# Windowed attention and eight experts on one core: the second expert product in plain f32, with tokens stationary

## The chip, the core and the metric

The kernel runs on one NeuronCore of a Trainium2 chip. Five engines work side by side: TensorE (PE in the rows; its weight loads are PEld), VectorE (DVE), ScalarE (ACT), GpSimd (POOL) and SyncE (SP, which here only starts transfers). The metric is the device time of one execution in microseconds; lower is better. All inputs lie in device memory in the layouts that the host prepares, and one launch does everything.

## The reference, cut to what matters

Eight batches of eight heads attend over a causal window of 64 positions. The result is laid out as 4608 tokens of 512 features, each token is sent to one of eight experts, and an expert keeps its 80 tokens of largest gate weight; all other rows of the output are zero.

```python
scores = scale * np.matmul(q, k.transpose(0, 1, 3, 2))     # 8 x 8 x 576 x 576, window of 64
attn = softmax(np.where(mask, scores, -1e9))
x = (attn @ v).transpose(0, 2, 1, 3).reshape(4608, 512)
expert_idx = np.argmax(x @ w_gate, axis=1)
for e in range(8):
    tok_idx = the 80 tokens of expert e with the largest gate weight
    h = np.maximum(x[tok_idx] @ w1[e], 0.0)                # 80 x 1024
    out[tok_idx] = gate_w[tok_idx, None] * (h @ w2[e])     # 80 x 512
```

## The kernel before

**Attention.** The tokens are worked on in 36 blocks of 128 (`unit`, `half`, `tail`): scores on TensorE in four tiles of 64 rows by 64 columns (L337), masking and maximum on VectorE (L350), the subtraction on GpSimd (L355), the exponential on ScalarE (L357), transposes (L366), the product with v in two column tiles (L417), then another transpose and the gate's logits in four column tiles of 32 (L444). Each finished block is written to `x_dram` (L379), and zeros are written to its rows of the output (L389). A routine called `list_schedule` works out beforehand in which order every engine's instructions are written down, from estimated durations; DMAs that SyncE starts are one of its queues. In it the first expert's weights are loaded in eight pieces of 512 KB (`first_weights`, L395 and L398). For a batch of 9 units of 64 tokens, q and k (L271) and v (L296, L302) are loaded into two buffers each, and GpSimd copies parts of v (L155).

**Routing** runs alongside and ends after the last block: ranks per expert in groups of blocks (`weigh`, `gate`, `merge`), and at the end `kept` (L585 to L598) with the list of 8 times 80 rows. While TensorE has little to do there, a job called `warm` puts in matmuls of an all-zero bf16 tile that nobody reads (L719). Another 28 of these (`WARM2`, L809) are written behind the gathers.

**Experts.** `gather` fetches an expert's 80 rows with an indirect DMA (L742), `load_x` turns them with four transposes (L769) and a copy (L770) so that features lie on partitions. `ffn1` computes h turned: the weights are stationary in two column tiles of 64, the 80 tokens stream past (64 matmuls in f32, each of which stands twice in the trace, L781). `ffn2` computes 80 tokens by 512 features with h stationary. It does not use f32 matmuls: `split` cuts w2 into a rounded part `wh` (ScalarE, L758) and the rest `wl` (VectorE, L759), h is cut in the same way (L783, L784), and three fp32r products per chunk of 128 are added up, 24 matmuls of 512 columns (L797). VectorE scales by the gate weight (L799), and an indirect DMA scatters the rows (L800). Two sets of weight buffers are in turn; expert e+2's load waits until expert e is done with its set. The order on TensorE is: transposes of e+1, second product of e, first product of e+1.

## Time and profile before

| | |
|---|---|
| median of 3 runs | 313.46 us (310.69 to 316.4) |
| the profiled execution | 313.2 us |
| its span, first to last instruction | 311.3 us |
| mean granted TensorE clock | 0.974 of full |
| TensorE busy | 279.2 us, 90% |
| moved by DMA | 84.32 MB |

The span falls into attention with routing beside it (to about 200 us), the end of the routing (to 214 us), the gather of the first expert's rows (to 217.7 us), and the experts (to 307 us), with the last scatter behind them. Times in the rows are microseconds from the start of the span. A matmul's own duration includes the way through the array, so matmuls that follow each other overlap, and the distance of their starts is what one costs.

### The profile page before, as it was taken

Reading aid. Unit: us, or ns where it says so; the run is one execution under the profiler, and the core shown is the slowest. Engines: PE = TensorE matmul, PEld = TensorE weight load, DVE = VectorE, ACT = ScalarE, POOL = GpSimd, SP = SyncE. Lnnn points to the kernel's source line nnn. Section 1 sums busy time; section 2 is a strip of 40 time slices with the busy share of each in tenths; the row PEclk is TensorE's granted clock in tenths of the full one; section 3 lists DMA queues with packets and bytes.
Section 4 is the critical chain, followed back from the end, with each engine's and each line's share of the span. In section 5 each row is a group of like instructions: output and inputs, shape, how many; then the busy total and the mean of one; then the engine's idle time right before and its main releaser. Section 6 shows DMA issues by size and latency. Waiting matters only on the chain. (4 is left out here: it accounts for less than half of the span.)

```text
span 311.3 us, 11705 instructions
## 1 busy us (share of the span) xinstructions
PE 279.2 (90%) x4706; PEld 221.2 (71%) x4706; DVE 220.6 (71%) x1084; ACT 157.2 (51%) x305; POOL 160.0 (51%) x255
## 2 busy tenths in 40 slices
PE   7699999888989998889997998895999999999983
PEld 5478787666866876667875876663977886787683
DVE  1358665677749857999799998984686466595471
ACT  1263876666565545766575667320555055145320
POOL 8899878698589579769766242003700101110111
PEclk9789999999999999999999999998699999999998
DMA  7978599889899958398371313991898999999400
GB/s 275 428 260 330 213 335 369 302 275 373 285 343 335 321 201 306 138 364 316 114 265 72 137 71 137 301 373 36 287 344 273 412 430 368 394 430 400 179 23 21
DMA packets 22245, 84.32 MB, mean 271 GB/s; under 512 B 2352, under 2 KB 2480, under 8 KB 18608
## 3 DMA queue, kind: packets, MB, share of 16 engines
q1 hardware_dynamic: 20736, 76.70, 66.4%
q10 hardware_dynamic: 432, 4.26, 4.2%
q0 software_dynamic: 1024, 2.62, 2.7%
q8 instruction: 37, 0.61, 0.8%
q14 instruction: 16, 0.13, 0.1%
HBM read 63.39 MB, written 20.19 MB: 269 GB/s over the span
## 5 line engine op out<-in xcount | busy, mean ns | idle before, releaser
L355 POOL TENSOR_TENSOR sm<-nb,sm 128x512 f32<-128x512 f32 x72 | 74.3, 1040 | 23.7 <-DVE nb L350 8.7
L357 ACT ACTIVATE sm<-sm 128x512 f32<-128x512 f32 x72 | 44.9, 633 | 37.5 <-POOL sm L355 37.1
L366 PE MATMUL pT_ps<-ident,sm 128*128 128x128 f32 x288 | 43.8, 284 | 5.9 <-ACT sm L357 4.9
L369 ACT COPY pT<-pT_ps 128x512 f32<-128x512 f32 x72 | 40.8, 586 | 11.6 <-PE pT_ps L366 11.0
L800 POOL DMA_INDIRECT out_dram<-y,dst_i x8 | 7.3, 919 | 75.8 <-DVE y L799 75.8
L759 DVE TENSOR_TENSOR wl<-w2t,wh 128x1024 fp32r<-128x1024 f32 x28 | 32.4, 1221 | 19.3 <-ACT wh L758 19.3
L337 PE MATMUL sc<-qkT 64*64 64x128 f32 x1152 | 42.7, 280 | 2.2 <-DVE nb L350 2.1
L155 POOL TENSOR_SCALAR vw<-vw 64x520 f32<-64x520 f32 x64 | 39.7, 621 | 9.4 <-DMA vw<-in_v_dram 5.9
L417 PE MATMUL o<-vw,pT 128*64 128x65 f32 x1152 | 42.3, 226 | 0.0
L417 PEld LDWEIGHTS o<-vw,pT 128*64 128x64 f32 x1152 | 37.2, 139 | 7.0 <-issue 5.3
L366 PEld LDWEIGHTS pT_ps<-ident,sm 128*128 128x128 f32 x288 | 32.8, 144 | 11.1 <-ACT sm L357 6.4
L337 PEld LDWEIGHTS sc<-qkT 64*64 64x64 f32 x1152 | 33.0, 135 | 9.2 <-issue 7.3
L758 ACT CAST wh<-w2t 128x1024 fp32r<-128x1024 f32 x28 | 27.2, 1046 | 15.4 <-DMA w2t<-in_w_dram 15.4
L350 DVE CUSTOM_DVE_ANT_0 sm<-sc,mask_oe 128x128 f32<-128x128 f32 x128 | 29.1, 286 | 6.8 <-PE sc L337 5.8
L781 PEld LDWEIGHTS hp<-xgT,w1t 128*64 128x64 f32 x896 | 31.4, 137 | 2.7 <-ACT wh L758 1.6
L781 PE MATMUL hp<-xgT,w1t 128*64 128x80 f32 x896 | 32.5, 233 | 0.0
L439 ACT COPY xT<-xT_ps 128x512 f32<-128x512 f32 x36 | 21.0, 583 | 19.7 <-PE xT_ps L436 19.4
L797 PE MATMUL yp<-wh,hh 128*80 128x512 f32 (+1 forms) x72 | 26.8, 372 | 1.0 <-DVE hh L783 0.9
L350 DVE CUSTOM_DVE_ANT_0 sm<-sc,mask_eo 128x128 f32<-128x128 f32 x96 | 21.8, 285 | 8.0 <-PE sc L337 7.9
L797 PE MATMUL yp<-wl,hh 128*80 128x512 f32 (+1 forms) x72 | 26.4, 367 | 0.0
L797 PE MATMUL yp<-wh,hl 128*80 128x512 f32 (+1 forms) x72 | 26.4, 367 | 0.0
L436 PE MATMUL xT_ps<-ident,xt 128*128 128x128 f32 x144 | 22.6, 279 | 3.6 <-DVE g L519 1.4
(132 smaller groups left out, 447.3 us busy)
## 6 DMA issues: line engine op xcount, KB each, us to landing
w1t<-in_w_dram SPq DMA_DIRECT2D x6, 2048.0 KB, 9.3
w2t<-in_w_dram SPq DMA_DIRECT2D x6, 2048.0 KB, 13.8
x_dram<-xt SPq DMA_DIRECT2D x36, 256.0 KB, 3.8
out_dram<-zeros SPq DMA_DIRECT2D x36, 256.0 KB, 4.4
qkT<-in_qk_dram SPq DMA_DIRECT2D x7, 1280.0 KB, 6.8
vw<-in_v_dram SPq DMA_DIRECT2D x7, 1040.0 KB, 6.7
qkT<-in_qk_dram SPq DMA_DIRECT2D x7, 1024.0 KB, 8.9
w<-in_w_dram SPq DMA_DIRECT2D x8, 512.0 KB, 6.6
```

The lines of the kernel that those rows point to most:

```text
L155: nc.gpsimd.tensor_scalar(dst, src, 1.0, 1.0, op0=ALU.mult, op1=ALU.mult)
L337: nc.tensor.matmul(scs[T][r][64 * m:64 * m + 64, pr, :], qkT[b][hp, i, pr, 0, :], kw, start=True, stop=True, tile_position=(64 * r, 64 * m))
L350: nc.vector.tensor_tensor_reduce(sm[:, pr], scs[T][r][:, pr], mask, op0=ALU.add, op1=ALU.min, scale=-0.125, scalar=-8.0 * NEG, accum_out=n ...
L355: nc.gpsimd.tensor_tensor(sm, nb.unsqueeze(2).broadcast_to([P, NP, P]), sm, op=ALU.subtract)
L357: nc.scalar.activation(sm, sm, AF.Exp)
L366: nc.tensor.transpose(tp[:, pr, :], sm[:, pr, :], ident)
L369: nc.scalar.copy(pT, tp)
L417: nc.tensor.matmul(ov[64 * m:64 * m + 64, h // 4, h % 4, :], pTs[T, h % 2][:, h // 2, 64 * m:64 * m + 64], vw[b][:, i, h, :], start=True, ...
L758: nc.scalar.copy(wh[:, f:f + 2, :], ws[e][1][:, f:f + 2, :])
L759: nc.vector.tensor_tensor(wl[:, f:f + 2, :], ws[e][1][:, f:f + 2, :], wh[:, f:f + 2, :].bitcast(F32), op=ALU.subtract)
L781: nc.tensor.matmul(hp[64 * m:64 * m + 64, f, :], ws[e][0][:, c, col:col + 64], xTs[e][:, c, :], start=(c == 0), stop=(c == KD - 1), tile_p ...
L797: nc.tensor.matmul(yp[:, 0:w], a[:, f, :], b[:, f, c:c + w], start=(f == 0 and i == 0), stop=(f == KF - 1 and i == 2))
```

## The change

The second product is taken in f32 from the unsplit w2. The tokens in h stay stationary. The first 64 of them go into the two halves of TensorE's columns, where half m produces output features 256 m to 256 m + 255 (`ya`); the other 16 go into the four quarters, where quarter m produces features 128 m to 128 m + 127 (`yb`). `split`, the second tile of h and the buffers for `wh` and `wl` are gone. VectorE scales the two halves; ScalarE scales the four quarters into rows 64 to 79. For that the gate weights are copied once to the partitions on which the parts come out (`gwa`, `gwb`). There are four sets of weights instead of two: the second expert's set is loaded during attention like the first, in eight more pieces. The first product of expert e+1 and the transposes of e+2 come ahead of the second product of e. The 28 matmuls of zeros are written by `warm` behind the end of the routing.

```diff
-    w_first = (w0.tile([P, KD, F], F32, name="w1_0"), w0.tile([P, KF, DM], F32, name="w2_0"))
+    w_first = [(w0.tile([P, KD, F], F32, name=f"w1_{i}"), w0.tile([P, KF, DM], F32, name=f"w2_{i}")) for i in range(2)]
...
         def first_weights(i):
-            yield f"?spill{i + 6}"
+            e, i = divmod(i, KD + KF // 2)
+            yield f"?spill{i + 6 + 10 * e}"
...
-        for i in range(KD + KF // 2):
+        for i in range(2 * (KD + KF // 2)):
             jobs.append((2 * i + 24, first_weights(i)))
...
+            left = WARM2
             for _ in range(1000 if end else WARM0):
-                if "kept" in state:
+                left -= "kept" in state
+                if left < 0:
                     break
...
-    wr = ctx.enter_context(tc.tile_pool(name="wr", bufs=2, reuse_waits="tile"))
+    ws = w_first + [(wt.tile([P, KD, F], F32, name=f"w1_{i}"), wt.tile([P, KF, DM], F32, name=f"w2_{i}"))
+                    for i in range(2, 4)]
...
     def weights(e, eng=nc.sync):
+        for t, w in zip(ws[e % len(ws)], (w1, w2)):
+            eng.dma_start(t, w[e])
...
-    def split(e, f0, f1):
...
-        nc.vector.tensor_scalar(hh[:, f0:f0 + 4, :], hp, 0.0, None, op0=ALU.max)
-        nc.vector.scalar_tensor_tensor(hl[:, f0:f0 + 4, :], hp, 0.0, hh[:, f0:f0 + 4, :].bitcast(F32),
-                                       op0=ALU.max, op1=ALU.subtract)
+        nc.vector.tensor_scalar(hs[e][:, f0:f0 + 4, :], hp, 0.0, None, op0=ALU.max)

     def ffn2(e):
...
-        w = DM if e + 1 < E else DM // 2
-        for c in range(0, DM, w):
-            yp = ps_y.tile([n_, DM], F32, name="yp")
+        def product(yp, k, x0, x1):
+            n = DM * k // P
             for f in range(KF):
-                for i, (a, b) in enumerate(((hh, wh), (hh, wl), (hl, wh))):
-                    nc.tensor.matmul(yp[:, 0:w], a[:, f, :], b[:, f, c:c + w], start=(f == 0 and i == 0),
-                                     stop=(f == KF - 1 and i == 2))
-            nc.vector.tensor_scalar(y[:, c:c + w], yp[:, 0:w], gw[:, e:e + 1], None, op0=ALU.mult)
+                for m in range(P // k):
+                    nc.tensor.matmul(yp[k * m:k * m + x1 - x0, :], h[:, f, x0:x1], w[:, f, n * m:n * m + n],
+                                     start=(f == 0), stop=(f == KF - 1), tile_position=(0, k * m))
+
+        product(ya, 64, 0, 64)
+        nc.vector.tensor_scalar(y[0:64, 0:DM // 2], ya[0:64], gw[0:64, e:e + 1], None, op0=ALU.mult)
+        nc.vector.tensor_scalar(y[0:64, DM // 2:DM], ya[64:128], gwa[64:128, e:e + 1], None, op0=ALU.mult)
+        product(yb, 32, 64, n_)
+        for m in range(4):
+            part = slice(32 * m, 32 * m + n_ - 64)
+            nc.scalar.activation(y[64:n_, P * m:P * m + P], yb[part], AF.Copy, scale=gwb[part, e:e + 1])
...
     with tc.manual_schedule():
-        weights(1)
+        weights(2)
         for e in range(E):
             gather(e)
-        t = ps_w.tile([P, 512], F32, name="warm")
-        for _ in range(WARM2):
-            nc.tensor.matmul(t[:, 0:WARMN], idle[:, 0:P], idle, start=True, stop=True)
         load_x(0)
...
         ffn1(0, 0)
-        split(0, 4, KF)
         ffn1(0, 4)
+        load_x(1)
         for e in range(E):
-            if e + 1 < E:
-                load_x(e + 1)
-                split(e + 1, 0, KF)
-            if 0 < e < E - 2:
-                weights(e + 2)
-            ffn2(e)
             if e + 1 < E:
                 ffn1(e + 1, 0)
                 ffn1(e + 1, 4)
+            if e + 2 < E:
+                load_x(e + 2)
+            ffn2(e)
+            if e + len(ws) < E:
+                weights(e + len(ws))
```

TensorE near the end of the routing, before. L719 and L809 are the matmuls of zeros, L444 the gate's logits, L675 a transpose of the routing:

```order
L719 LDWEIGHTS idle
L719 MATMUL warm<-idle 128x256
L444 MATMUL lg<-xT,wgp 32x128 x4
L809 LDWEIGHTS idle
L809 MATMUL warm<-idle 128x256
...
L675 LDWEIGHTS st
L675 MATMUL vp<-ident_b,st 24x80
```

The 28 of L809, though written behind the gathers, stand between the routing's matmuls in the built program; only three of L719 stand behind the routing's last one. The same place and the place behind the routing's last matmul (L663) in the changed program, on the same engine, where L722 writes all matmuls of zeros:

```order
L722 LDWEIGHTS idle
L722 MATMUL warm<-idle 128x256
L445 MATMUL lg<-xT,wgp 32x128 x4
L676 LDWEIGHTS st
L676 MATMUL vp<-ident_b,st 24x80
...
L663 MATMUL ns<-st,oho 80x6
L722 LDWEIGHTS idle
L722 MATMUL warm<-idle 128x256
...
L766 MATMUL tp<-ident,xg 128x80 x4
```

None of the 28 stands between the routing's matmuls now; 31 stand in a row behind the last one, ahead of the first expert's transposes (L766).

TensorE in the experts, before (tp are transposes, hp a first product, yp a second):

```order
L769 MATMUL tp<-ident,xg 128x80 x4
L781 MATMUL hp<-xgT,w_0_145 64x80 x64
L769 MATMUL tp<-ident,xg 128x80 x4
L797 MATMUL yp<-wh,hh 80x512
L797 MATMUL yp<-wl,hh 80x512
L797 MATMUL yp<-wh,hl 80x512
...
L781 MATMUL hp<-xgT,w1t 64x80 x64
```

And in the changed program, from the first expert's transposes on:

```order
L766 MATMUL tp<-ident,xg 128x80 x4
L777 MATMUL hp<-xgT,w_0_145 64x80 x64
L766 MATMUL tp<-ident,xg 128x80 x4
L777 MATMUL hp<-xgT,w_1_147 64x80 x64
L766 MATMUL tp<-ident,xg 128x80 x4
L791 MATMUL ya<-w_0_146,h 64x256 x16
L791 MATMUL yb<-w_0_146,h 16x128 x32
L777 MATMUL hp<-xgT,w_2_4606 64x80 x64
```

Two first products now stand ahead of the first second product, with one set of transposes straight ahead of the second of them; every later set of transposes has a second product behind it.

SyncE's queue in the middle of attention in the changed program (L396 and L399 are the pieces of the second expert's weights, the others as before):

```order
L379 DMA x_dram<-xt 128x512
L396 DMA w_1_147<-in_w_dram 128x1024
L389 DMA out_dram<-zeros 128x512
L379 DMA x_dram<-xt 128x512
L271 DMA qkT<-in_qk_dram 128x2560
L379 DMA x_dram<-xt 128x512
L271 DMA qkT<-in_qk_dram 128x2048
L396 DMA w_1_147<-in_w_dram 128x1024
L399 DMA w_1_148<-in_w_dram 128x1024
```

The eight new pieces stand between the blocks' writes, the loads of q, k and v and the zeros, and some of the zeros stand later than before. On VectorE and ScalarE the order of attention and routing is unchanged; on TensorE one set of transposes and on GpSimd one copy of v stands a place earlier.

## Rows read from the trace of the kernel before

**Rows 1.** The head of the page: span, busy time of each engine, and the granted clock in tenths in 40 slices of 7.8 us.

```profile
span 311.3 us, 11705 instructions
PE 279.2 (90%) x4706; PEld 221.2 (71%) x4706; DVE 220.6 (71%) x1084; ACT 157.2 (51%) x305; POOL 160.0 (51%) x255
...
PEclk9789999999999999999999999998699999999998
```

**Rows 2.** Busy time by stretch: start and end, length, busy time (and instructions) of PE, PEld, DVE, ACT and POOL, then the granted clock, the DMA's share and GB/s. First a part of the attention, then the experts 1 to 6.

```profile
100.00:150.00 50.00, 45.24 (x880) 36.24 (x875) 41.81 (x258) 30.80 (x67) 39.18 (x59) 1.00 0.74 266
...
224.00:290.00 66.00, 65.88 (x986) 51.49 (x981) 45.60 (x59) 26.14 (x31) 6.40 (x7) 1.00 0.98 382
```

**Rows 3.** The same columns in short stretches around the end of the routing.

```profile
207.00:209.00 2.00, 1.72 (x14) 0.93 (x13) 1.86 (x13) 0.71 (x3) 0.00 (x0) 1.00 1.01 434
214.30:216.00 1.70, 0.00 (x0) 0.00 (x0) 0.60 (x5) 0.00 (x0) 1.29 (x2) 1.00 0.00 0
216.00:218.00 2.00, 0.34 (x3) 0.37 (x4) 0.00 (x0) 0.00 (x0) 1.69 (x2) 0.57 0.52 137
220.00:222.00 2.00, 2.00 (x36) 2.00 (x34) 1.55 (x2) 2.00 (x3) 1.70 (x2) 0.50 0.78 287
224.00:226.00 2.00, 2.00 (x48) 1.82 (x43) 2.00 (x3) 0.14 (x1) 0.88 (x1) 1.00 1.13 385
```

**Rows 4.** Instructions in order of time at the hand-over to the experts: start, duration, engine, line, operation, and in brackets the idle time ahead of it with what ended it.

```profile
213.76 0.49 PE L719 MATMUL warm<-idle 128*128 128x256 bf16 x3
214.40 1.16 POOL L742 DMA_INDIRECT xg<-x_dram,src_i  x1 [24.18 <-DVE val L587]
217.66 0.77 PE L769 MATMUL tp<-ident,xg 80*128 80x80 f32 x4 [3.41 <-DMA xg<-x_dram,src_i]
218.24 0.29 ACT L770 COPY xgT<-tp 128x160 f32<-128x160 f32 x1 [7.04 <-PE tp L769]
218.58 6.81 PE L781 MATMUL hp<-xgT,w 128*64 128x80 f32 x128 [0.16 <-ACT xgT L770]
225.33 0.50 PE L769 MATMUL tp<-ident,xg 80*128 80x80 f32 x4
```

**Rows 5.** The same view for one undisturbed expert: its first product, transposes, the first and the last matmul of the second product, and the next expert's first product.

```profile
241.79 4.65 PE L781 MATMUL hp<-xgT,w1t 128*64 128x80 f32 x128
246.37 0.50 PE L769 MATMUL tp<-ident,xg 80*128 80x80 f32 x4
246.66 0.44 PE L797 MATMUL yp<-wh,hh 128*80 128x512 f32 x1
246.96 0.43 ACT L770 COPY xgT<-tp 128x320 f32<-128x320 f32 x1 [6.32 <-PE tp L769]
251.77 0.39 PE L797 MATMUL yp<-wl,hh 128*80 128x512 f32 x1
252.00 0.39 PE L797 MATMUL yp<-wh,hl 128*80 128x512 f32 x1
252.32 4.65 PE L781 MATMUL hp<-xgT,w1t 128*64 128x80 f32 x128
```

**Rows 6.** f32 matmuls in column tiles during attention, in order of time: 128 columns past four tiles of 128 rows by 32 columns (L444) and of 64 by 64 (L337), and what follows them on TensorE.

```profile
103.78 0.64 PE L444 MATMUL lg<-xT,wgp 128*32 128x128 f32 x16
...
109.16 0.43 PE L444 MATMUL lg<-xT,wgp 128*32 128x128 f32 x8
109.52 1.10 PE L337 MATMUL sc<-qkT 64*64 64x128 f32 x32
110.56 0.33 PE L452 MATMUL lg<-ident,ls 128*128 128x128 f32 x1
```

**Rows 7.** Groups of instructions, by line and form: count, then busy time and mean duration (ns) of one, then idle time ahead of them and what ended it. VectorE's part of the splits, two f32 matmuls in column tiles, and a small copy on ScalarE.

```profile
L759 DVE TENSOR_TENSOR wl<-w2t,wh 128x1024 fp32r<-128x1024 f32 x28 | 32.4, 1221 | 19.3 <-ACT wh L758 19.3
L781 PE MATMUL hp<-xgT,w1t 128*64 128x80 f32 x896 | 32.5, 233 | 0.0
L337 PE MATMUL sc<-qkT 64*64 64x128 f32 x1152 | 42.7, 280 | 2.2 <-DVE nb L350 2.1
L450 ACT COPY ls<-lg 128x128 f32<-128x128 f32 x4 | 1.0, 262 | 2.5 <-PE lg L444 2.5
```

**Rows 8.** The last two experts in order of time, to the last scatter.

```profile
283.92 4.65 PE L781 MATMUL hp<-xgT,w1t 128*64 128x80 f32 x128
294.76 4.65 PE L781 MATMUL hp<-xgT,w1t 128*64 128x80 f32 x128
300.32 0.32 PE L797 MATMUL yp<-wh,hh 128*80 128x256 f32 x1 [0.91 <-DVE hh L783]
306.08 0.28 PE L797 MATMUL yp<-wh,hl 128*80 128x256 f32 x1
306.40 0.48 DVE L799 TENSOR_SCALAR y<-yp,gw 80x256 f32<-80x256 f32 x1 [2.31 <-PE yp L797]
307.16 0.91 POOL L800 DMA_INDIRECT out_dram<-y,dst_i  x1 [6.19 <-DVE y L799]
```

**Rows 9.** Transfers by kind: count, size of one, and median time from issue to landing; w2t are the second halves of the later experts' weights, w the pieces of the first expert's.

```profile
w2t<-in_w_dram SPq DMA_DIRECT2D x6, 2048.0 KB, 13.8
w<-in_w_dram SPq DMA_DIRECT2D x8, 512.0 KB, 6.6
```

**Rows 10.** Who waited for whom: GpSimd's copies of v for the load; us in total, times, longest.

```profile
POOL vw L155 <- DMA vw<-in_v_dram: 5.9, 5, 2.2
```

More of the change, by code (lines that the diff above doesn't have):

```diff
@@ L729, in attn_moe @@
     src_i, dst_i, gw = state["kept"]
-    wt = ctx.enter_context(tc.tile_pool(name="wt", bufs=2, reuse_waits="tile"))
-    wr = ctx.enter_context(tc.tile_pool(name="wr", bufs=2, reuse_waits="tile"))
+    wt = ctx.enter_context(tc.tile_pool(name="wt", bufs=1, reuse_waits="tile"))
     fk = ctx.enter_context(tc.tile_pool(name="fk", bufs=2, reuse_waits="tile"))
@@ L735, in attn_moe @@
     ps_y = ctx.enter_context(tc.tile_pool(name="ps_y", bufs=2, space=PSUM))
-    ps_w = ctx.enter_context(tc.tile_pool(name="ps_w", bufs=1, space=PSUM))
+    ps_z = ctx.enter_context(tc.tile_pool(name="ps_z", bufs=2, space=PSUM))
     n_ = CAP
-    xgs, ws, hs, xTs, wsp = {}, {0: w_first}, {}, {}, {}
+    xgs, hs, xTs = {}, {}, {}
+    ws = w_first + [(wt.tile([P, KD, F], F32, name=f"w1_{i}"), wt.tile([P, KF, DM], F32, name=f"w2_{i}"))
+                    for i in range(2, 4)]
+    gwa = fk.tile([P, E], F32, name="gwa", bufs=1)
+    gwb = fk.tile([P, E], F32, name="gwb", bufs=1)
     def gather(e):
@@ L746, in weights @@
     def weights(e, eng=nc.sync):
-        w1t = wt.tile([P, KD, F], F32, name="w1t")
-        eng.dma_start(w1t, w1[e])
-        w2t = wt.tile([P, KF, DM], F32, name="w2t")
-        eng.dma_start(w2t, w2[e])
-        ws[e] = w1t, w2t
-    def split(e, f0, f1):
-        if f0 == 0:
-            wsp[e] = (wr.tile([P, KF, DM], F32R, name="wh"), wr.tile([P, KF, DM], F32R, name="wl"))
-        wh, wl = wsp[e]
-        for f in range(f0, f1, 2):
-            nc.scalar.copy(wh[:, f:f + 2, :], ws[e][1][:, f:f + 2, :])
-            nc.vector.tensor_tensor(wl[:, f:f + 2, :], ws[e][1][:, f:f + 2, :], wh[:, f:f + 2, :].bitcast(F32),
-                                    op=ALU.subtract)
+        for t, w in zip(ws[e % len(ws)], (w1, w2)):
+            eng.dma_start(t, w[e])
     def load_x(e):
@@ L773, in ffn1 @@
         if f0 == 0:
-            hs[e] = (fk.tile([P, KF, n_], F32R, name="hh"), fk.tile([P, KF, n_], F32R, name="hl"))
-        hh, hl = hs[e]
+            hs[e] = fk.tile([P, KF, n_], F32, name="h")
         hp = ps_h.tile([P, 4, n_], F32, name="hp")
@@ L780, in ffn1 @@
                     col = P * (f0 + f) + 64 * m
-                    nc.tensor.matmul(hp[64 * m:64 * m + 64, f, :], ws[e][0][:, c, col:col + 64], xTs[e][:, c, :],
+                    nc.tensor.matmul(hp[64 * m:64 * m + 64, f, :], ws[e % len(ws)][0][:, c, col:col + 64], xTs[e][:, c, :],
                                      start=(c == 0), stop=(c == KD - 1), tile_position=(0, 64 * m))
-        nc.vector.tensor_scalar(hh[:, f0:f0 + 4, :], hp, 0.0, None, op0=ALU.max)
-        nc.vector.scalar_tensor_tensor(hl[:, f0:f0 + 4, :], hp, 0.0, hh[:, f0:f0 + 4, :].bitcast(F32),
-                                       op0=ALU.max, op1=ALU.subtract)
+        nc.vector.tensor_scalar(hs[e][:, f0:f0 + 4, :], hp, 0.0, None, op0=ALU.max)
@@ L787, in ffn2 @@
     def ffn2(e):
[L788 to L789 removed]
+        h, w = hs[e], ws[e % len(ws)][1]
         y = fk.tile([n_, DM], F32, name="y")
[L792 to L794 removed]
+        ya = ps_y.tile([P, DM // 2], F32, name="ya")
+        yb = ps_z.tile([P, DM // 4], F32, name="yb")
+        def product(yp, k, x0, x1):
+            n = DM * k // P
             for f in range(KF):
[L796 to L799 removed]
+                for m in range(P // k):
+                    nc.tensor.matmul(yp[k * m:k * m + x1 - x0, :], h[:, f, x0:x1], w[:, f, n * m:n * m + n],
+                                     start=(f == 0), stop=(f == KF - 1), tile_position=(0, k * m))
@@ L803, in attn_moe @@
     with tc.manual_schedule():
-        weights(1)
+        weights(2)
         for e in range(E):
             gather(e)
-        t = ps_w.tile([P, 512], F32, name="warm")
-        for _ in range(WARM2):
-            nc.tensor.matmul(t[:, 0:WARMN], idle[:, 0:P], idle, start=True, stop=True)
         load_x(0)
-        weights(2, nc.scalar)
-        split(0, 0, 4)
+        for e in range(3, len(ws)):
+            weights(e, nc.scalar)
+        nc.vector.tensor_copy(gwa[64:128], gw[0:64])
+        for m in range(4):
+            nc.vector.tensor_copy(gwb[32 * m:32 * m + n_ - 64], gw[64:n_])
         ffn1(0, 0)
-        split(0, 4, KF)
         ffn1(0, 4)
+        load_x(1)
         for e in range(E):
-            if e + 1 < E:
-                load_x(e + 1)
-                split(e + 1, 0, KF)
-            if 0 < e < E - 2:
-                weights(e + 2)
-            ffn2(e)
             if e + 1 < E:
```

6 lines of the change are left out of this document (2 added, 4 removed).

## The prediction

> **What bounds the kernel now.** I read the page first, then stretches, then single instructions. TensorE is busy for 90% of the span, and its granted clock is full but for a stretch near the start, one at about 220 us and the end [rows 1]. In the experts it is busy for 65.88 of 66.00 us [rows 2]: VectorE's splits (32 instructions of 1.22 us with the first expert's), ScalarE's and the weights (DMA share 0.98) all lie beside it. So what the change takes from VectorE, ScalarE and DMA there is worth nothing by itself. What counts is how long TensorE needs for an expert, and what stands at the two ends of that stage, where TensorE does wait: the gather, and the last expert.
>
> One expert takes 252.32 - 241.79 = 10.53 us [rows 5]: first product 4.58 (241.79 to 246.37), transposes 0.29, second product 5.66, of which the last 0.32 is one matmul (0.23, the distance of starts) and 0.09 for the change to half columns. At the hand-over the clock falls: TensorE has nothing to do from 214.25 until the gather lands at 217.66, the granted clock is 0.57 and then 0.50 of full (the 1.2 GHz level), and is full again only after 224 [rows 3, 4]. The first expert's first product therefore takes 225.33 - 218.58 = 6.75 us in place of 4.58 [rows 4]. At the other end the last second product starts at 300.32, after TensorE sat idle for 0.91 us for h; it is done in halves by about 306.36, VectorE scales until 306.88, and the scatter goes out at 307.16 [rows 8].
>
> **What a second product costs in f32.** Its form is not in the trace; two neighbours are. Each f32 matmul stands there twice. In L337 32 of them, 128 columns past four tiles, take 1.10 us with a last one of 0.28, so (1.10 - 0.28) / 31 = 26 ns each, 106 ns for a round of four [rows 6, 7]. In L781 128 of them, 80 columns past two tiles, take (4.65 - 0.23) / 127 = 34.8 ns each, 70 ns for a round of two [rows 5, 7]. So tiles stream side by side, and a round costs 0.83 to 0.87 ns per column, about two periods of 2.4 GHz. That L444, with tiles of all 128 rows and 32 columns, keeps this up is in its 16: (0.64 - 0.28) / 15 = 24 ns each [rows 6]. The halves `ya` are 16 matmuls of 256 columns, 32 in the trace, 16 rounds of 2 x 106 = 212 ns: 3.39 us. The quarters `yb` are 32 of 128 columns, 64 in the trace, 16 rounds of 106: 1.70 us. To this come the changes of tiling. L337's group holds TensorE from 109.52 to 110.56, 1.04 us for 8 rounds that make 0.85: 0.19 for starting and changing [rows 6]. I take 0.19 for `ya`, 0.19 for `yb` and 0.09 behind the transposes. The second product then costs 3.58 + 1.89 = 5.47, and an expert 4.58 + 0.38 + 5.47 = 10.43 us, against 10.53. **Per expert nearly nothing is won.** The three fp32r products were as cheap as the f32 ones in tiles are. Bounds: extended by the slope between the two neighbours, (106 - 70) / 48 = 0.75 ns per column, a round of 256 is 202 ns, and with no price on changes the second product is 4.93 us; with L781's 34.8 ns for each of the 64 quarter matmuls, as if issue and not streaming set the pace, and 0.19 twice, it is 6.0 us.
>
> The tiling's modes change twice more per expert. By the rows the next group starts before the previous ends (L337 at 109.52, while L444 that began at 109.16 lasts 0.43, so 0.07 earlier [rows 6]). The Trainium skill's page "TensorEngine Tiling (Array Packing)", section "Key Properties", says that changing the mode, unlike changing the tile, drains TensorE. Were that a full wait for the end, each of the four changes of an expert would cost 0.07 more, 2.2 us over eight experts, and the sum below would be 0.7% longer; the row shows an overlap, so I keep the row.
>
> **The hand-over.** The 28 matmuls of zeros leave the routing and stand, with three others, in a row ahead of the first transposes. At full clock one takes (0.49 - 0.27) / 2 = 0.11 us, so 31 last from 213.76 to 217.1, and the gather lands just behind at 217.66 [rows 4]. I expect a full clock there: transposes and copy 0.13 shorter, and the first product starts at 218.45 and ends at 223.03 in place of 225.33. That the routing keeps its clock without the 28 is read from 207 to 209, where none of the 28 ran and the clock was 1.00 [rows 3]. New is a bubble: the second transposes now have the first product of expert 1 straight behind them, which waits for their copy. From transposes to copied is 246.37 to 247.39 [rows 5], so 1.1 us with the hand-over, and expert 1's first product starts at 224.13. The five small copies of gate weights on VectorE (an estimate of 0.2 each, below the 0.26 of ScalarE's copy of 128 columns [rows 7]) lie beside the first product.
>
> **From there to the end** TensorE has no wait that I can find: 7 first products 32.06, 6 transposes 2.28, 8 second products 43.76, to 302.23, the last result 0.2 later. Weights are early: a set that comes free has three experts' time, some 30 us, where w2t lands in 13.8 [rows 9], and the wait for h is gone, since another expert's second product lies between. Then four scalings on ScalarE follow each other, 0.26 for the first and some 0.22 for each further one [rows 7]: 303.4, in place of VectorE's 306.88. The scatter behind them is as before. That is **3.5 us earlier**: 2.3 from the clock, 1.1 from the last wait and about 0.3 from the stall ahead of 294.76 (10.84 from 283.92 in place of 10.53 [rows 8]), 0.4 from the last product's halves, 0.7 from the second products, less 0.8 for the bubble and 0.5 for ScalarE at the end.
>
> **Attention.** Eight pieces of 512 KB, 4.2 MB, enter SyncE's queue between about 104 and 147 us. From 100 to 150 the DMA's share is 0.74 at 266 GB/s [rows 2]; 4.2 MB more make 350 GB/s, below the 382 of the experts' stage. By that rate a piece is 1.4 us, during which what stands behind it waits. GpSimd, in order, already waits up to 2.2 us for v [rows 10], and the queue puts two blocks of zeros closer ahead of one load of v. Bounds: nothing (loads run a batch ahead; a small gain from the shifted places is possible, -0.5), and 4 us, if half the pieces reach a wait with 1.0 to 1.4 us each. I take 0.5, near the lower end, since the first expert's pieces already run among the same kinds of transfers and land in 6.6 us [rows 9], and all five waits of GpSimd for v together are 5.9 us.
>
> **The sum** against the profiled execution: 313.2 - 3.5 + 0.5 = **310.2 us**. The median of the three runs is 313.46, 0.3 above that execution, so this is 1.0% less.
>
> **Rivals.**
> - *The second product is dearer* (chance 0.18): drains, or the quarters' pace set by issue, up to 6.0 us in place of 5.47. Eight times 0.5 is 4.2, which takes the gain: 312 to 314.5. For it: 16 columns stationary are a form that no row has. Against: 24 and 26 ns in the two four-tile rows.
> - *The clock is lost anyway* (0.07). Without the 28 the stretch from 200 to 206 is thinner; were the clock halved when the 31 zeros start, they would last 6.6 us, to 220.4, hold the transposes back by 2.7 and the first product would still be slow: about 314. Against it stands the full clock from 207 to 209.
> - *Slower: the quarters do not run four abreast* (0.08). If 128 rows of w2 for four tiles at once cannot be fed for long, and two go abreast, `yb` costs 16 rounds of 212 ns, 3.39 in place of 1.70; eight times 1.7 is 13.5: 323.7. It decides from an excess of about 1.2 us per expert on. Against it is L444 with the same tiles, though for 16 only.
> - *Attention pays in full* (0.07): 4 us and more, 314 to 317.
> - *The cheap end* (0.15): second product 4.93 and nothing lost in attention, 4.3 + 0.5 less: 305.4, with values down to there from 308.
> - That loads come late in spite of four sets, or that the order isn't the written one, I give nothing: the order shows the products ahead.
>
> **How the numbers follow.** The forecast holds 0.45, its own range 308 to 312.5. "Within 2%" is 307.2 to 319.7, about what a measurement of this kernel can tell from no change. Faster takes the cheap end and some of the forecast's lower edge, 0.2; slower takes the quarters two abreast and a little of attention, 0.1; the same 0.7. The range 305.8 to 314.8 leaves out the slow quarters and attention's upper end.
>
> **What would show it.** Right: `ya` in 3.4 to 3.6 us and `yb` in 1.7 to 1.9 per expert, 10.3 to 10.6 from one first product to the next, a first first product of 4.6 us at clock 1.00, a gap of 0.7 to 0.9 us ahead of expert 1's first product, no wait for weights, and the gather starting within 1 us of 214.40. Wrong: the clock at 0.50 at 218; quarter matmuls more than 35 ns apart; the gather's start over 2 us later, which would be attention.

## The result, and the profile after

The changed kernel takes **314.81 us** (median of 20 runs, 311.53 to 318.06), the kernel before beside it 312.98 (20 runs, 310.69 to 316.4): ratio 1.0072, 95% interval 1.0049 to 1.0094. The forecast was 310.2 us, a small gain; measured is a small loss, just above the upper end of the range. The profiled execution has a span of 312.9 us against 311.3 [rows 1].

The head of the changed kernel's page, as in [rows 1], with the line of the queue that carries instructions (packets, MB, share of the engines):

```profile
span 312.9 us, 12779 instructions
PE 281.2 (90%) x5258; PEld 222.9 (71%) x5258; DVE 179.2 (57%) x1048; ACT 137.4 (44%) x305; POOL 159.5 (51%) x255
...
PEclk9699999999999999999999999959999899999998
...
q8 instruction: 41, 0.67, 0.8%
```

VectorE and ScalarE lost the splits' work, and TensorE has more matmuls, 5258 for 4706. PEclk has a 5 at the end of the routing (the slice from 203 us), where it had none before, and one dip in the experts, later than before. Busy time by stretch, columns as in [rows 2]: a part of the attention, the experts, and the end of the routing [rows 3].

```profile
100.00:150.00 50.00, 45.43 (x879) 36.41 (x877) 41.51 (x259) 31.14 (x67) 39.08 (x59) 1.00 0.95 338
224.00:290.00 66.00, 62.88 (x1304) 51.20 (x1304) 10.92 (x23) 9.74 (x26) 4.62 (x5) 0.97 0.84 317
203.00:206.00 3.00, 2.02 (x18) 1.20 (x19) 2.86 (x15) 0.21 (x1) 0.00 (x0) 0.73 1.10 466
206.00:209.00 3.00, 2.78 (x23) 1.79 (x21) 2.25 (x10) 0.73 (x2) 0.00 (x0) 0.50 0.65 279
209.00:212.00 3.00, 3.00 (x23) 2.02 (x23) 1.97 (x10) 0.21 (x1) 0.00 (x0) 0.63 0.01 3
```

Two things stand there that the prediction does not have: TensorE is idle for 3.1 us in the experts, and the routing runs at half clock from 206 to 209 (0.50, the 1.2 GHz level). The instructions in order of time, from the first gather to expert 3 (L766 transposes, L777 first products, L791 second products):

```profile
213.55 1.17 POOL L751 DMA_INDIRECT xg<-x_dram,src_i  x1 [24.85 <-PE warm L722]
...
216.85 0.47 PE L766 MATMUL tp<-ident,xg 80*128 80x80 f32 x4 [0.41 <-DMA xg<-x_dram,src_i]
217.61 4.65 PE L777 MATMUL hp<-xgT,w 128*64 128x80 f32 x128 [0.29 <-ACT xgT L767]
222.19 0.50 PE L766 MATMUL tp<-ident,xg 80*128 80x80 f32 x4
223.20 4.72 PE L777 MATMUL hp<-xgT,w 128*64 128x80 f32 x128 [0.52 <-ACT xgT L767]
227.85 0.50 PE L766 MATMUL tp<-ident,xg 80*128 80x80 f32 x4
228.28 3.67 PE L791 MATMUL ya<-w,h 128*64 128x256 f32 x32
231.88 1.48 PE L791 MATMUL yb<-w,h 128*16 128x128 f32 x42
233.75 0.84 PE L791 MATMUL yb<-w,h 128*16 128x128 f32 x22 [0.38 <-issue]
234.52 3.88 PE L777 MATMUL hp<-xgT,w 128*64 128x80 f32 x105
241.13 1.18 PE L777 MATMUL hp<-xgT,w 128*64 128x80 f32 x23 [2.74 <-issue]
242.24 0.80 PE L766 MATMUL tp<-ident,xg 80*128 80x80 f32 x4
242.97 4.81 PE L791 MATMUL ya<-w,h 128*64 128x256 f32 x32
247.71 1.94 PE L791 MATMUL yb<-w,h 128*16 128x128 f32 x64
249.59 4.65 PE L777 MATMUL hp<-xgT,w 128*64 128x80 f32 x128
```

The hand-over is as forecast: the first product starts 0.76 us behind the start of the transposes and lasts 4.58, not 6.75 [rows 4]. Then TensorE stops twice in the middle of a run of matmuls whose operands have long been there; "issue" means that the profile shows nothing that it waits for. Behind the longer stop the granted clock falls to 0.50, and `ya` takes 4.74 in place of 3.60. From 234.52 to 249.59 are 15.07 us, where the next expert takes 10.47 (249.59 to 260.06) and the later ones 10.48.

The end, to the last scatter, as in [rows 8]:

```profile
305.01 1.94 PE L791 MATMUL yb<-w,h 128*16 128x128 f32 x64
307.07 1.47 ACT L800 ACTIVATE y<-yb,gwb 16x128 f32<-16x128 f32 x4 [4.00 <-issue]
```

The scatter starts at 308.81, where it started at 307.16.

### The profile page after: what moved, and what is told of

Its sections match the earlier page's. It is cut to its first block, busy times and chain, and to the rows that moved or that the text cites. A ratio compares the mean times of both kernels' runs of the same rounds, so it can differ in the third digit from the quotient of the medians.

```text
span 312.9 us, 12779 instructions
## 1 busy us (share of the span) xinstructions
PE 281.2 (90%) x5258; PEld 222.9 (71%) x5258; DVE 179.2 (57%) x1048; ACT 137.4 (44%) x305; POOL 159.5 (51%) x255
## 4 chain that ended last, share of the span: by engine, by line
PE 52%; DVE 21%; POOL 12%; issue 7%; DMA 3%; ACT 3%; POOLq 0%; DVEq 0%; ACTq 0%
PE hp L777 12%; PE ya L791 9%; PE sc L337 6%; PE o L418 6%; DVE sm L350 5%; POOL sm L355 5%; PE yb L791 4%; PE pT_ps L366 4%; POOL vw L155 4%; DVE ahead L575 3%; DMA vw<-in_v_dram 2%; PE xT_ps L437 2%; PE lg L445 2%; DVE xt L428 2%; DVE oho L653 2%
## 5 line engine op out<-in xcount | busy, mean ns | idle before, releaser
L337 PE MATMUL sc<-qkT 64*64 64x128 f32 x1152 | 43.4, 283 | 2.2 <-issue 1.2
L777 PE MATMUL hp<-xgT,w 128*64 128x80 f32 x1024 | 37.7, 234 | 3.5 <-issue 2.7
L337 PEld LDWEIGHTS sc<-qkT 64*64 64x64 f32 x1152 | 33.5, 137 | 9.4 <-issue 7.2
L777 PEld LDWEIGHTS hp<-xgT,w 128*64 128x64 f32 x1024 | 36.2, 137 | 5.2 <-issue 4.1
L779 DVE TENSOR_SCALAR h<-hp 128x320 f32<-128x320 f32 x16 | 7.9, 492 | 41.2 <-PE hp L777 41.2
L800 ACT ACTIVATE y<-yb,gwb 16x128 f32<-16x128 f32 x32 | 11.5, 359 | 45.0 <-PE yb L791 32.3
L791 PE MATMUL ya<-w,h 128*64 128x256 f32 x256 | 30.5, 392 | 0.0
L428 DVE TENSOR_TENSOR xt<-o,r 128x512 f32<-128x512 f32 x36 | 24.8, 690 | 0.7
L791 PEld LDWEIGHTS ya<-w,h 128*64 128x64 f32 x256 | 18.2, 141 | 9.5 <-issue 1.3
```

Of the source, the lines that this page charges most:

```text
L337: nc.tensor.matmul(scs[T][r][64 * m:64 * m + 64, pr, :], qkT[b][hp, i, pr, 0, :], kw, start=True, stop=True, tile_position=(64 * r, 64 * m))
L428: nc.vector.tensor_tensor(xt, ov[:, :, :, 0:D], r.unsqueeze(3).broadcast_to([P, 2, 4, D]), op=ALU.mult)
L777: nc.tensor.matmul(hp[64 * m:64 * m + 64, f, :], ws[e % len(ws)][0][:, c, col:col + 64], xTs[e][:, c, :], start=(c == 0), stop=(c == KD - ...
L791: nc.tensor.matmul(yp[k * m:k * m + x1 - x0, :], h[:, f, x0:x1], w[:, f, n * m:n * m + n], start=(f == 0), stop=(f == KF - 1), tile_positi ...
```

## The experiments

Two theories were put up. **Theory 1:** TensorE runs out of program, since its next piece is fetched beside the weights. An instruction packet has 16,384 bytes; 41 of them for 5258 matmuls and as many weight loads (37 for 4706 before) make some 256 instructions a packet, or 128 matmuls with their loads. Between the two stops lie 22 + 105 = 127 matmuls. **Theory 2:** the routing loses its clock because the 28 zeros that ran among its steps are gone.

**Without the late weights.**

```
-            if e + len(ws) < E:
-                weights(e + len(ws))
```

> The changed kernel without the loads of experts 4 to 7 (their products run on the weights of experts 0 to 3, so their rows are not the reference's); the order on TensorE is unchanged. Theory: in expert 2's first product TensorE runs out of instructions, because the next 16 KB of its program wait in the DMA engines behind weight transfers. Then the stop of 2.7 us and the half clock behind it are gone, the time from expert 2's first product to expert 3's falls from 15.1 to about 10.5 us, and the kernel takes about 310 us, 1% less than the kernel before. Rival: TensorE waits there for something of the kernel's own (PSUM, h, the turned rows). Then the stop stays and the time stays near 314.5.

312.29 us, ratio 0.9958 (0.992 to 0.9995). Expert 2, in order of time:

```profile
236.74 4.65 PE L777 MATMUL hp<-xgT,w 128*64 128x80 f32 x128
241.31 0.50 PE L766 MATMUL tp<-ident,xg 80*128 80x80 f32 x4
241.74 3.67 PE L791 MATMUL ya<-w,h 128*64 128x256 f32 x32
245.34 1.94 PE L791 MATMUL yb<-w,h 128*16 128x128 f32 x64
```

The long stop is gone (10.47 us to the next expert); the short one, 0.38, stands, while set 3 is still loading. Expert 2's operands and instructions are the same, so the stop comes from the transfers. The 310 us did not come: in this trace the gather starts at 215.60, 2.05 later than in the changed kernel's, with the routing at half clock for longer.

**All weights on one queue**: `w1` of expert 4, then set 3, on SyncE's queue behind the first products; none on ScalarE's.

> The changed kernel with all weight loads of the experts' stage on SyncE's queue: expert 3's set is no longer started by ScalarE at 217 us but by SyncE behind the first half of expert 4's. The bytes are the same. If the instructions come late because two queues of weights stand in the DMA engines at once, the stop is gone: 10.5 us from expert 2's first product to expert 3's, about 310 us. If a full DMA as such delays them (its share stays near 1.0 until 250 us), a stop stays, here or a block later, and the time is 312 to 315.

314.0 us, ratio 1.0031 (0.9985 to 1.0076). The stop is at the same matmul and lasts 0.73, with 0.34 and 0.60 further on; the clock of the experts stays at 1.00. Why it is shorter is taken up with the table of packets below. The gather came late, at 215.60, with half clock from 203 to 212.

**The program moved.** `WARM2 = 12` for 28.

> The changed kernel with 12 in place of 28 matmuls of zeros behind the routing, so all later instructions of TensorE stand 32 places earlier in the program. If TensorE stops at the end of a block of its program, the stop moves by 16 matmuls: from behind 105 of expert 2's first product to behind about 121, and the short one in the quarters from behind 42 to behind about 58. If it waits for data, the stop stays behind the 105th. The row of zeros ends 1.7 us earlier; I expect no lost clock from that.

One run, 314.93 us. Expert 2 has its stop 16 matmuls later, after 121:

```profile
236.11 4.43 PE L777 MATMUL hp<-xgT,w 128*64 128x80 f32 x121
242.40 0.49 PE L777 MATMUL hp<-xgT,w 128*64 128x80 f32 x7 [1.86 <-issue]
```

It goes with the place in the program, not with the product, a tile or a time. The short stop, expected behind 58 of the quarters, is not in this trace. Even with 12 zeros for 28 the hand-over has full clock, but the routing lost its clock, which was not expected.

**The kernel before with its zeros moved behind the routing**, the rest as it was.

> The kernel before with one part of the change alone: the 28 matmuls of zeros stand behind the routing. Theory: the first expert's first product runs at full clock, 4.6 in place of 6.75 us, and the kernel takes 2.0 to 2.5 us less, about 310.6. Rival: the routing, thinner now, loses the clock and gives it back, so that the time is within 0.5 us of the kernel before.

314.69 us in 4 runs (310.81 to 317.41): no verdict. Its trace has half clock from 205.6 to 212.5 and 15.67 us from the last token rows (the last write to `x_dram`) to the gather, where the kernel before has 14.94. So the loss in the routing comes with the zeros' move and not with the rest of the change; so does the gain at the hand-over:

```profile
218.06 4.65 PE L783 MATMUL hp<-xgT,w 128*64 128x80 f32 x128 [0.29 <-ACT xgT L772]
```

**Smaller pieces.**

```
-        for t, w in zip(ws[e % len(ws)], (w1, w2)):
-            eng.dma_start(t, w[e])
+        t1, t2 = ws[e % len(ws)]
+        for c in range(KD):
+            eng.dma_start(t1[:, c], w1[e, :, c])
+        for c in range(0, KF, 2):
+            eng.dma_start(t2[:, c:c + 2], w2[e, :, c:c + 2])
```

> The changed kernel with every set of weights that the expert stage loads (sets 2 and 3 of the start, and the four late ones) sent as eight transfers of 512 KB instead of two of 2 MB, on the same queues at the same places. In the changed kernel these transfers move in packets of 16 KB; pieces of 512 KB move in packets of 4 KB, as those of the first two sets do in the attention. Theory 1 (TensorE runs out of program: the next piece of it is fetched behind the packets of the weights): the fetch waits behind shorter packets, the stop of 2.74 us in expert 2's first product shrinks to under 1 us, the clock stays at 1.00 there, experts 1 to 2 take 10.5 to 11.5 us instead of 15.1, and the span is 3 to 4.5 us shorter than 312.9. Rival A (it is the number of bytes in flight that holds up the fetch, not the size of the packets): the stop stays between 2 and 3 us and the span within 1 us. Rival B (the stop is something of TensorE's own at this place): the same as A, but then the kernel without late loads would have stopped as well. The half clock in the routing should be as it was in all theories.

323.97 us, ratio 1.037 (1.029 to 1.0451), a miss for every theory. ScalarE's own work, with the time that it spent in issues (ACTq):

```profile
219.93 2.13 ACTq L758 DMA_DIRECT2D w<-in_w_dram  x4
222.16 11.93 ACTq L760 DMA_DIRECT2D w<-in_w_dram  x4
234.13 0.43 ACT L770 COPY xgT<-tp 128x320 f32<-128x320 f32 x1 [14.21 <-DMA w<-in_w_dram]
```

ScalarE stood in the issues of the last four pieces until 234.1, and the copy of the second tile, for which TensorE waits, stood behind them: 9.56 us of idle TensorE, then half clock. That earlier pieces had to go first is likely, but no run tests it. The size of the pieces isn't tested by this run.

**More zeros in the routing**: two in each place.

```
+                zt = bank_tile("t", [P, 512], F32, "warm")
+                for _ in range(2 if end and "kept" not in state else 1):
+                    nc.tensor.matmul(zt[:, 0:WARMN], idle[:, 0:P], idle, start=True, stop=True)
```

> The changed kernel with two zero products instead of one in each place where zeros are put between the steps of the routing (39 more; those behind the routing stay). Theory 2 (the routing of the changed kernel falls to half clock because the 28 zeros that ran among its steps are gone): the granted clock stays at 1.00 from 203 to 212 us, and from the last write of the token rows to the first gather it takes 14.9 us as before the change instead of 15.6 to 17.0. Rival (the routing waits for VectorE, GpSimd and ScalarE in a chain, and TensorE's clock costs it nothing): the clock is 1.00 but the gather starts no earlier. By theory 1 the two stops in the experts move back by 39 products: from after 42 of expert 0's quarters to after 3, and from after 105 to after 66 of expert 2's first product, with about the same length. Span 311 to 312.5 by theories 1 and 2, 312.9 by the rival.

315.77 us, ratio 1.0089 (1.005 to 1.0128). The clock is 1.00 throughout, yet from token rows to gather it takes 15.85: the last counting product (L663) stands behind 16 zeros, and VectorE waits 1.31 for it instead of 0.61. The stops in order of time:

```profile
227.28 3.33 PE L779 MATMUL hp<-xgT,w 128*64 128x80 f32 x89 [0.17 <-issue]
...
241.59 2.37 PE L779 MATMUL hp<-xgT,w 128*64 128x80 f32 x62 [2.58 <-issue]
...
253.97 1.46 PE L779 MATMUL hp<-xgT,w 128*64 128x80 f32 x34 [0.65 <-issue]
```

The long one is after 66 of 128, as expected. The other two, after 39 of expert 1's and 94 of expert 3's first product, lie two packets of 128 matmuls ahead of it and two behind it, counted through transposes, halves and quarters; at the places between, in the quarters of experts 0 and 1, nothing was held up this time. That the first stop would be after 3 of expert 0's quarters did not come.

**Pieces and more zeros together.**

> Both edits together: weights of the expert stage in pieces of 512 KB, and two zeros in each place of the routing. Theories 1 and 2 together: no stop over 1 us in the experts, clock 1.00 from 203 us to the end, gather 14.9 us behind the last token rows, and a span of 307 to 309 us, faster than the kernel before by 0.8 to 1.5%. If either theory falls, its part is missing: 311 to 312 us without the first, 308.5 to 310 without the second.

325.63 us, ratio 1.0406 (1.0339 to 1.0473): ScalarE's queue again, 11.01 us of idle TensorE.

**The kernel before with 28 zeros more**, behind the routing; the others stay.

> The kernel before with 28 more zeros, behind the routing and ahead of the first expert; the 28 that run among the routing's steps stay. This is the hand-over's part of the change by itself, with the second products, weights and buffers as they were. If the prediction's step for the hand-over is right: full clock at the first product (4.65 us instead of 8.8), routing at full clock, gather 14.9 us after the last token rows, and 2 to 2.5 us less than before. Rival (the split of the first expert's second weights or the load of weights then ends later than TensorE, so the gain is given back at the second products): the first product is short but a new wait of 1.5 us or more stands before the second product or in expert 1. By theory 1 a stop for program can occur here too, since the second weights of the experts are loaded in the same large packets.

311.43 us, ratio 0.9943 (0.9901 to 0.9984). The first product has full clock (217.92, 4.65 long; before it took 6.81 [rows 4], not the 8.8 of the expectation) and from token rows to gather it takes 14.94. In the trace the gain, 2.5 us at expert 1's first product, is spent later:

```profile
266.74 0.43 PE L799 MATMUL yp<-wh,hh 128*80 128x512 f32 x1 [1.30 <-DVE hh L785]
...
300.36 0.32 PE L799 MATMUL yp<-wh,hh 128*80 128x256 f32 x1 [2.28 <-DVE hh L785]
```

TensorE waits for VectorE, behind whose splits stand, and starts the last second product at 300.36, where it was 300.32 [rows 8]. The rival of this expectation held for the profiled execution; over the timed runs a gain of 0.6% stays.

**More zeros early only**: two for the first 26 places, one for the last thirteen.

> The changed kernel with two zeros instead of one in the first 26 places of the routing only, so that the last thirteen places, ahead of the last counting product, stay as in the change. By theory 2 the clock stays at 1.00 from 203 us on, and without the 0.9 us that the doubled zeros held up the last counting product the gather starts 14.9 us after the last write of the token rows, as in the kernel before. Rival (the routing takes its 15.6 us or more for another reason): 15.6 to 17. By theory 1 the stop in expert 2's first product moves from after 105 of 128 to after 79, and keeps about its length; the span is 312.9 less 0.7, if the last token rows come as early as in the changed kernel's trace.

315.22 us (4 runs), ratio 1.0118 (1.0015 to 1.022). The routing, columns as above:

```profile
203.00:206.00 3.00, 2.00 (x24) 1.59 (x24) 2.84 (x16) 0.84 (x3) 0.00 (x0) 1.00 1.03 421
206.00:209.00 3.00, 2.75 (x25) 1.81 (x24) 2.81 (x16) 0.94 (x3) 0.00 (x0) 1.00 1.01 431
209.00:212.00 3.00, 3.00 (x37) 2.44 (x35) 2.06 (x11) 0.21 (x1) 0.00 (x0) 1.00 0.12 46
```

From token rows to gather: 15.01, as before the change (14.94). The stops stay, after 16 of expert 0's quarters (0.68) and after 79 of expert 2's first product (2.87), both places 26 earlier, as expected. The median shows no gain from the routing here (the changed kernel has 1.0072).

**One queue, set 3 straight behind set 2.**

> As the run before it, and weight set 3 goes on SP's queue behind set 2, so that ScalarE issues no weights and one queue carries them all. Theory 1 (the fetch of TensorE's program waits its turn among the weight queues): the stops of expert 0 to 4 together come to 0.7 to 2 us instead of 3.1, none is long enough to halve the clock, and with the routing at full clock the span is 308.5 to 310.0 us; the median 1 to 3 us below the kernel before. Rival (the routing's half clock is not what was lost): 310.5 to 311.5.

318.68 us, ratio 1.0191 (1.0103 to 1.0279), a miss. TensorE's first transposes:

```profile
223.28 0.77 PE L768 MATMUL tp<-ident,xg 80*128 80x80 f32 x4 [6.34 <-DMA xg<-x_dram,src_i]
```

The gather started in time, at 214.05, but set 3 now fills the DMA when it moves (share 1.01 from 212 to 215, where the changed kernel has 0.02), and lands 6 us late; the clock is lost with it. The stops are as hoped: 0.3 us in all.

**The same in pieces.**

> As the run before it, with the weights in pieces of 512 KB (packets of 4 KB) on SP's queue. The pieces issued by ScalarE were what made the earlier kernel with pieces slow (ScalarE sat in an issue of 11.93 us, and the next token tile's copy behind it); SP has no other work, so here a full queue costs nothing. Theory 1 with size of packets as the cause: no stop over 0.3 us, span 308 to 309. Rival (bytes in flight, not the size of a packet): stops as with one queue and large packets, 0.7 to 2 us together.

316.42 us, ratio 1.0138 (1.0052 to 1.0225): the transposes at 220.50, the same trouble, and stops of 0.58 and 0.19.

**Two of the last four scalings on VectorE**, on the kernel with set 3 behind set 2.

> The kernel with early zeros and one queue, and of the last expert's four scalings of the quarters VectorE does two, beside ScalarE's two. In the changed kernel ScalarE's four took 1.47 us in a row between the last product and the last scatter, where the prediction had 0.95. Two a side: about 0.75 us, so the last scatter starts 0.6 to 0.8 us sooner after the last product. Rival (the reads of one PSUM bank by two engines are served in turn): still 1.3 to 1.5 us.

318.77 us, ratio 1.0194 (1.0111 to 1.0278). The last scalings, VectorE's and ScalarE's:

```profile
311.72 0.34 DVE L803 TENSOR_SCALAR y<-yb,gwb 16x128 f32<-16x128 f32 x1 [1.29 <-ACT y L805]
312.50 0.36 DVE L803 TENSOR_SCALAR y<-yb,gwb 16x128 f32<-16x128 f32 x1 [0.43 <-ACT y L805]
```

They take turns, each waiting for the other over `y`, the one tile that all write; nothing is won. Whether the bank would have served both isn't told by this.

**Early zeros, one queue, set 3 behind the first late load.**

```
+                for _ in range(2 if end and k < 26 else 1):
...
-        for e in range(3, len(ws)):
-            weights(e, nc.scalar)
...
         ffn1(0, 4)
+        nc.sync.dma_start(ws[0][0], w1[4])
+        weights(3)
         load_x(1)
```

> Two zeros in the first 26 places of the routing, and weight set 3 on SP's queue behind the first late load, which waits for the first expert's first product; so it does not meet the gather, ScalarE issues no weights, and one queue carries all. Theories 1 and 2: gather 14.9 us behind the last token rows, first product at full clock, stops of expert 0 to 4 together 0.7 to 1.7 us as in the run with one queue, none that halves the clock; span 309.5 to 310.5, median 0 to 2 us below the kernel before. Rival (more is lost than these two): span over 311.

**311.38 us** (12 runs, 310.3 to 311.95), ratio 0.9971 (0.9938 to 1.0004), span 310.1. Gather 15.01 behind the token rows, first product at full clock, full clock to the last scatter. Experts 2 to 4 take 10.76, 11.71 and 10.98 us, 2.0 in all over 10.48 each, a little more than expected; the longest stop:

```profile
249.92 0.98 PE L779 MATMUL hp<-xgT,w 128*64 128x80 f32 x21 [0.95 <-issue]
```

**That in pieces of 512 KB.**

> As the run before it, with the weights of sets 2 to 7 in pieces of 512 KB (packets of 4 KB instead of 16 KB) on the same queue in the same order. If the size of the packets is what holds up TensorE's program: stops under 0.3 us together, span 0.7 to 1.5 us shorter than the run before it. If it is the bytes in flight: the same stops within 0.3 us and the same span.

312.29 us, ratio 0.9995 (0.9958 to 1.0032), span 310.6. At the same matmul:

```profile
249.80 0.97 PE L782 MATMUL hp<-xgT,w 128*64 128x80 f32 x21 [1.58 <-issue]
```

Over 10.48 each, the experts lose 3.0 us here. Smaller packets do not shorten the stops, so their size is not the cause; that the weights' traffic as such is, rests on the runs without late weights.

**Early zeros, no late weights.**

> The changed kernel with two zeros in the first 26 places of the routing and without the loads of experts 4 to 7's weights (these experts use the weights of experts 0 to 3, so their outputs are other numbers; the work of every engine but the transfers is the same). The sum of the two failed steps: against the changed kernel 0.7 us from the routing's clock and 4.6 us from the longer stop and the half clock behind it, so about 307.6 us of span if the last token rows come at 197.9 us, later by as much as these come later; the median 308 to 310, where the prediction had 310.2. Rival (a third loss is still unseen): span over 309.5.

309.77 us, ratio 0.9919 (0.988 to 0.9958), span 307.3, every expert from 2 on 10.48 us. Without the stops and with the routing's clock the forecast (310.2) is met, so beside ScalarE's end no third loss of any size is left. It is met by leaving out transfers that the kernel needs, so this run sizes the loss and is no way to avoid it.

**The last expert's quarters ahead of its halves**, on the kernel with set 3 late.

> The kernel with early zeros and weight set 3 late on one queue, and for the last expert the quarters go ahead of the halves: ScalarE's four scalings (1.47 us) then lie beside TensorE's halves (3.6 us), and behind the last product stand VectorE's two (0.97 us) alone. If the scalings were path: the last scatter starts 1.0 us after the last product instead of 1.5, the span is 0.4 to 0.6 us shorter than 310.1, and the median 1.5 to 2.5 us below the kernel before. Rival (the halves read the quarters' result late, or the two engines' writes to one tile are ordered): VectorE waits for ScalarE and the end is as before.

318.51 us where the kernel before took 316.5, ratio 1.0077 (1.0037 to 1.0118). The profiled execution took 324.3 us, with 3.6 us of stops in the first product, so its trace says little of the median. These six stops come after 38, 42, 45, 46, 48 and 49 matmuls, not 128 apart, so theory 1 does not explain them. Its end can be read: the last product ends at 316.55 and the scatter starts at 318.43, 1.88 later, as with ScalarE last (304.11 to 305.98). A miss; why VectorE's shorter end wins nothing, and why the kernel is slower than the one it is made from (timed on another chip), stays open.

## Why the prediction was wrong, and where it was right

**Right: the products.** `ya` 3.60, `yb` 1.88, an expert 10.48, where 3.58, 1.89 and 10.43 stood. The neighbours of [rows 6] were the right price, and the rivals on the quarters fall. The Trainium skill's page "TensorEngine Tiling (Array Packing)", section "Key Properties", says that changing the tiling mode drains TensorE. Were each of the four changes of an expert a full wait, as the prediction priced it, 0.28 more should stand there; 0.05 does, and by the rows each group still starts 0.07 before the one ahead of it ends (`ya` from 254.59 lasts 3.67, `yb` starts at 258.19). A shorter drain could hide in the 0.47 that the sum has for changes.

**Right: the hand-over.** From the gather to the end of the first product 8.64 us (forecast 8.63, before 10.93), the bubble behind it 1.01 (1.1).

**Not seen: attention's 0.5 us.** Its DMA share went from 0.74 to 0.95, yet the last token rows came at 197.93, before the change at 199.46. Over the runs but the last they came between 197.9 and 200.0 with the second set's loads in the attention (198.8 in the mean of 14 traces), and between 198.3 and 199.5 without (198.9, three traces). That the changed kernel's trace has the earliest of all is luck.

**Wrong: "the routing keeps its clock without the 28".** The row from 207 to 209 [rows 3] was read as a stretch without zeros. It was a stretch just behind them: in the trace of before 27 of the 28 ran between 200.3 and 206.3, the last at 206.8. Some of them, and the clock of that stretch, before the change:

```profile
200.26 0.93 PE L809 MATMUL warm<-idle 128*128 128x256 bf16 x7
...
204.97 1.36 PE L809 MATMUL warm<-idle 128*128 128x256 bf16 x11
...
206.77 0.27 PE L809 MATMUL warm<-idle 128*128 128x256 bf16 x1
...
206.00:209.00 3.00, 2.72 (x30) 1.76 (x28) 2.79 (x19) 0.71 (x3) 0.00 (x0) 1.00 1.01 435
```

Without them the same three microseconds have 0.50, and the routing takes 0.7 to 2.1 us longer. From the last token rows to the gather, over all kernels but the last:

| | us |
|---|---|
| clock 1.00: the kernel before, it with 28 zeros more, and the seven with more early zeros | 14.94 to 15.02 |
| clock 0.50 in part: changed kernel, zeros behind, 12 zeros | 15.62, 15.67, 16.03 |
| clock 0.50 for longer: no late weights, one queue, pieces | 16.89, 17.00, 17.01 |
| clock 1.00, but two zeros in every place (two kernels) | 15.85 |

In timed runs the ratio falls with the early zeros by 0.4% without late weights (0.9958 to 0.9919) and by 0.6% with one queue (1.0031 to 0.9971), but the intervals of each pair overlap, and with two queues nothing was gained (1.0118 for 1.0072): this part of the loss is shown by the traces, not by the medians. The rival "the clock is lost anyway" had the right place and cause, but not the end: the clock came back before the hand-over. That its 314 us is close to the measured time is luck.

**Wrong, and the larger part: "TensorE has no wait that I can find".** The prediction looked for operands, buffers and engines. The program itself was late. Tiles of half and quarter width make 228 matmuls of an expert (128 + 4 + 32 + 64) where there were 156 (128 + 4 + 24), in the same 10.5 us: a packet of 128 lasts 5.9 us, before 8.6. The starts of the instruction packets (queue q8) in the traces say how fast they come:

| while | apart, us |
|---|---|
| hardly any weights move (early zeros, no late weights: 233.20, 236.88; DMA share 0.16) | 3.7 |
| one queue of weights (set 3 late: 228.49 to 259.93, six packets) | 6.1 to 6.5 |
| one queue in pieces (227.81 to 259.88, six packets) | 6.1 to 6.9 |
| two queues (changed kernel: 223.35, 231.20, 238.55) | 7.9, 7.4 |
| the same packets, one queue (all weights on one queue: 222.97, 230.93, 238.10) | 8.0, 7.2 |

In these stretches beside the weights a packet comes later than TensorE needs one (single ones came closer, 4.4 behind 257.73 in the changed kernel, but 6.4 in the mean from 250.03 to 269.29); what had been fetched ahead is used up by expert 0's quarters. The number of queues does not space them: with all weights on one queue the first of the three came 3.2 us behind the first product's start, where it came 5.7 behind in the changed kernel, whose set 3 was already moving. That fits its shorter stop. The packets also say where each stop ends. Over all traces there are 21 stops called "issue" in the experts (the last run's first product apart), and every one ends 2.4 to 2.7 us behind the start of an instruction packet; in the changed kernel 233.75 is 2.55 behind 231.20, and 241.13 is 2.58 behind 238.55. Before the change a packet was needed every 8.6 us and came every 6.0 to 6.2 where wanted (245.55, 251.79, 257.82), and its trace has no such stop. That the two stops and the half clock behind them are most of the miss is in the sum: they cost 4.6 us in expert 2 and 0.8 in expert 0, and the last result came 83.8 us behind expert 1's start where 78.3 were forecast. In the timed runs, taking out the late loads alone moves the ratio from 1.0072 (at least 1.0049) to 0.9958 (at most 0.9995).

**Wrong in size: ScalarE's end.** Four scalings take 1.47 us, 0.36 each, and not 0.26 and three times 0.22. The price was that of a plain copy of 128 columns [rows 7]; these are activations with a scale for each row, which no row had, and one behind the other they do not get shorter. 0.5 us.

So against the forecast scatter, 3.0 earlier than before, it came 1.65 later: 5.4 in the experts, 0.6 for the end, less 1.35 because the gather was 0.85 earlier and not 0.5 later (the routing's 0.7 in it, and the luck of early token rows).

## What to carry to other kernels

When a rewrite cuts products into more and shorter matmuls at equal time, count instructions as well as columns: TensorE's program comes through the same DMA as the weights, so an engine whose operands are all early can still stand still, and the profile calls that "issue". Here the full clock from 207 to 209 was lost when work from 200 to 207 was taken out, so when work is taken out, read the stretches ahead of the row too. And a load that fills the DMA or an engine's queue is placed by what it meets, the gather or the next copy, not only by when its data are needed.

## What the runs showed of the hardware

- The next 128 matmuls' worth of TensorE's program came 3.7 us apart on a nearly idle DMA and 6.1 to 8.0 us apart in the table's stretches beside weights. Neither weights in packets of 4 KB for 16 KB (6.1 to 6.9 for 6.1 to 6.5) nor one queue for two (8.0 and 7.2 for 7.9 and 7.4) brought it sooner.
- A stop for program ended 2.4 to 2.7 us behind the start of the next packet of it, in 21 of 21 stops.
- A stop of 2.74 us was followed by half clock in the changed kernel; stops of 2.58 and 2.87 elsewhere were not.
- ScalarE, issuing eight transfers of 512 KB in a row, spent 2.13 us on the first four and 11.93 us on the other four, with its own work behind them.
